# An attention and MLP kernel: casts moved from ScalarE to GpSimd, attention tiles issued in pairs ahead of the MLP, and the last output tile in two banks

## The chip, the cores and the metric

The kernel runs on one core of a Trainium2 chip. The metric is the device time of one execution in microseconds. In the text PE is TensorE (PEld its weight loads), DVE is VectorE, ACT is ScalarE, POOL is GpSimd, SP is SyncE, whose queue issues most DMAs. "fp32r" is the reduced float32 type in which TensorE multiplies faster than in plain float32. L595 means line 595 of the kernel.

## The reference

Sliding-window attention with sink keys, followed by a two-layer MLP, everything in float32 from the outside:

```python
# q, k, v: (4, 8, 768, 64); n_sink = 4, window = 128
scores = q @ k.T / 8
keep = (key < n_sink) | ((0 <= row - key) & (row - key < window))
a = softmax(where(keep, scores, -1e9))
x = (a @ v), heads side by side           # (3072, 512)
h = x @ w_in                              # w_in (512, 2048), given as float64
out = maximum(0.01 * h, h) @ w_out        # w_out (2048, 512), given as float64
```

## The kernel before

**Tiling.** The 3072 tokens are cut into eight units `u` of 384 tokens (half a sequence, T = 3 tiles of 128 rows). A unit is attended in four pairs of heads, then goes through the MLP in 16 chunks `fc` of 128 hidden columns. Precision is kept by splitting: a float32 operand becomes a high part (a cast to fp32r) and a low part (the difference), and a product is three fp32r matmuls: high x high, high x low, low x high. So every weight tile has `hi` and `lo` (L180, L181), every attention output `xh` and `xl` (`emit_x`, L548), every hidden chunk `gh` and `gl` (L604, L605).

**Weights.** They come as float64 and are decoded by three integer instructions on DVE (L172, L174, L176), then cast (ACT) and subtracted (POOL). `load_weights` brings them one tile at a time, alternately of `w_in` and `w_out`.

**Attention of the first two units** (`early_stream`, plain float32 matmuls). A tile is `(u, pair, j)`. Its `score` step is two matmuls (one for each head) into two PSUM banks (`pair_banks`), on DVE the mask, scale and row minimum in one instruction for each head (L303), on ACT the exponential (L305); for `u = 1` also the normalisation on ACT (L484). The probabilities stand in a buffer `pe` of which there are three (`PKB`). Its `turn` step transposes the probabilities on PE into a bank (`tail_pair`, L354, L355), which ACT copies out as `pt` (L357, L360). When the three tiles of a pair have been turned, `gather` (`sinks`) transposes the sink columns, which POOL copied aside (L358), and `value` (`values_pair`) multiplies with V. For `u = 0` the sums are applied after that: POOL spreads them (`rs`, L398), PE transposes them (L431), ACT copies them (L432), DVE multiplies (`xf`, L434), and `emit_x` makes `xh` on ACT (L551) and `xl` on DVE (L552).

**Order.** PE's order is the order in which the program is written; the other engines' instructions are ordered by a planner that simulates the kernel, within the limits of data and buffers. The attention is a generator that yields after every step. The first `early_steps + LEAD0` = 39 steps run ahead of the MLP (`phase[0]` is 0); score tiles then alternate between the bank pairs (s, o0) and (o1, o2), and transposes between banks h and t. Later steps are dealt out between the MLP's steps, at a rate worked out from the step counts. A `turn` follows its `score` by `SAHEAD` = 2 tiles; between the two stand the value group that is pending. Ahead of the MLP stand so 17 scores, 14 turns and the four value groups of unit 0, and four weight tiles are loaded there.

**MLP.** A chunk is 12 matmuls of 384 columns into one bank (L595), then `g` on ACT and DVE (L602, L603), `gh` on ACT, `gl` on POOL for unit 0 and on DVE for the others, and, one chunk later, for each of the three token tiles three matmuls of 512 columns that accumulate into the tile's bank o0, o1 or o2 (L619). After the last chunk the banks are copied out by DVE and stored. For the very last tile the last chunk's three matmuls are made in two halves of 256 columns in the same bank, one half copied by ACT and stored from ACT's queue, the other by DVE and stored from SP's.

Of the kernel before, what the change touches and what calls it, by code (L numbers as in the profile page):

```python
# [9 lines left out]
F32 = mybir.dt.float32  # L10
# [10 lines left out]
P = 128  # L21
# [6 lines left out]
T = 3  # L28
# [13 lines left out]
DEEP = 9.0e8  # L42
SO = 3
LEAD = 12
LEAD0 = 7
SAHEAD = 2
NACT = 4
LAG = 2
# [70 lines left out]
def fast_path(ctx, tc, cpool, qp, qk, vu, vs, w_in, w_out, out, ident, wz, lims, negm, wmin, wmax):  # L119
# [43 lines left out]
    def load_weights():  # L163
        fc, nm = len(wts) // 2, "io"[len(wts) % 2]
        raw = wpool.tile([P, 512, 2], I32, tag=f"w{nm}{fc}", name=f"w{nm}raw{fc}")
        dma = fetch(raw, nm, fc)
        pace(dma, decoded[-DEPTH] if len(decoded) >= DEPTH else anchors[-min(PRED, len(anchors))])
        top, low = raw[:, :, 1], raw[:, :, 0]
        word = ps_t.tile([P, 512], I32, tag="d", name=f"d{nm}{fc}")
        w = iopool.tile([P, 512], F32, tag="io", name=f"w{nm}f{fc}")  # L170
        with tc.issue_after(anchor[0].ins):
            nc.vector.tensor_scalar(out=word, in0=top, scalar1=3, scalar2=0x3FFFFFFF,  # L172
                                    op0=ALU.logical_shift_left, op1=ALU.bitwise_and)
        nc.vector.scalar_tensor_tensor(out=word, in0=top, scalar=-0x40000000, in1=word,  # L174
                                       op0=ALU.bitwise_and, op1=ALU.bitwise_or)
        decoded.append(nc.vector.scalar_tensor_tensor(out=w.bitcast(I32), in0=low, scalar=29, in1=word,  # L176
                                                      op0=ALU.logical_shift_right, op1=ALU.bitwise_or))
        both = wpool.tile([P, 2, 512], F32R, tag=f"w{nm}{fc}", name=f"w{nm}{fc}")
        hi, lo = both[:, 0, :], both[:, 1, :]
        nc.scalar.copy(out=hi, in_=w)  # L180
        nc.gpsimd.tensor_tensor(out=lo, in0=w, in1=hi.bitcast(F32), op=ALU.subtract)  # L181
        wts[nm, fc] = (hi, lo)

# [280 lines left out]
    def early_stream(pend):  # L464
# [2 lines left out]

        def score(u, pair, j):
            if j == 0:
                live[u, pair] = st = dict(raw=raws.pop((u, pair)), v=vraws.pop((u, pair)))  # L470
                load_next(u, pair)
                st["sk"] = apool.tile([P, T, 2, NSK], F32, tag="sk", name=f"sk{u}_{pair}")
                st["sm"] = apool.tile([P, 2, T], F32, tag="sm", name=f"sm{u}_{pair}", bufs=4)
                st["pt"] = apool.tile([P, 2, 2 * TU], F32, tag="pt", name=f"pt{u}_{pair}")
            st = live[u, pair]
            st["w", j] = w = apool.tile([P, 2, W3], F32, tag="pk", name=f"pe{u}_{pair}_{j}", bufs=PKB)
            softmax_pair(u, pair, j, scores_pair(u, pair, j, st["raw"]), w, st["sm"])
            sm = st["sm"][:, :, j] if u else st["sm"]
            if u or j == T - 1:
                nc.vector.tensor_scalar(out=sm, in0=sm, scalar1=1e-9, scalar2=None, op0=ALU.add)  # L480
                nc.vector.reciprocal(out=sm, in_=sm)
            if u:
                for x in range(2):
                    nc.scalar.mul(w[:, x, :], w[:, x, :], st["sm"][:, x, j:j + 1])  # L484
# [6 lines left out]
            live[u, pair]["st"] = sinks(u, pair, live[u, pair]["sk"], live[u, pair])  # L491

        def value(u, pair):
            values_pair(u, pair, live.pop((u, pair)))
            n = u * NPAIR + pair + 2
            if n < EARLY * NPAIR:
                load_values(*divmod(n, NPAIR))

        for k, tile_ in enumerate(tiles):
            score(*tile_)  # L500
            yield
            while pend:
                pend.pop(0)[1]()
                yield
            if k >= SAHEAD:
                u, pair, j = tiles[k - SAHEAD]
                turn(u, pair, j)
                yield
                if j == T - 1:
                    gather(u, pair)  # L510
                    yield
                    pend.append((1, lambda u=u, pair=pair: value(u, pair)))
        for u, pair, j in tiles[len(tiles) - SAHEAD:]:
            pend.append((0, lambda u=u, pair=pair, j=j: turn(u, pair, j)))
        pend.append((0, lambda: gather(u, pair)))
# [32 lines left out]
    def emit_x(u, pair, x):  # L548
        xh = xpool.tile([P, TU], F32R, tag=f"xh{pair}", name=f"xh{u}_{pair}")
        xl = xpool.tile([P, TU], F32R, tag=f"xl{pair}", name=f"xl{u}_{pair}")  # L550
        nc.scalar.copy(out=xh, in_=x)  # L551
        (nc.gpsimd if EARLY <= u < XLP else nc.vector).tensor_tensor(out=xl, in0=x, in1=xh.bitcast(F32), op=ALU.subtract)  # L552
        xs[u].append((xh, xl))

# [23 lines left out]
    def mlp_stream():  # L578
        po = {}
        prev = None  # L580
        for step in range(NU * NFC + 1):
            u, fc = divmod(step, NFC)
            cur = None
            if u < NU:
# [17 lines left out]
                nc.scalar.mul(g, ph[:, 0:TU], 0.01)  # L602
                anchor[0] = nc.vector.tensor_tensor(out=g, in0=ph[:, 0:TU], in1=g, op=ALU.max)  # L603
                nc.scalar.copy(out=gh, in_=g)  # L604
                (nc.gpsimd if u == 0 else nc.vector).tensor_tensor(out=gl, in0=g, in1=gh.bitcast(F32), op=ALU.subtract)  # L605
                cur = (u, fc, gh, gl)
                yield
            if prev is not None:
                v, f, gh, gl = prev
                if f == 0:  # L610
                    po = [ps_o.tile([P, 512], F32, tag=f"o{t}", name=f"o{v}_{t}") for t in range(T)]
                wh, wl = wts["o", f]
                for t in range(T):
                    tsl = slice(t * P, (t + 1) * P)
                    halves = 2 if (v, f, t) == (NU - 1, NFC - 1, T - 1) else 1
                    for x in range(halves):
                        cs = slice(x * 512 // halves, (x + 1) * 512 // halves)
                        for c, (gg, w) in enumerate(((gh, wh), (gh, wl), (gl, wh))):
                            nc.tensor.matmul(po[t][:, cs], lhsT=gg[:, tsl], rhs=w[:, cs], start=f == 0 and c == 0,  # L619
                                             stop=f == NFC - 1 and c == 2 and x == halves - 1)  # L620
                    if f == NFC - 1:
                        last = v == NU - 1 and t == T - 1
                        r0 = (v * T + t) * P
                        if last:
                            obs = [apool.tile([P, 256], F32, tag="stg", name=f"ob{v}_{t}_{x}") for x in range(2)]
                            nc.scalar.copy(out=obs[0], in_=po[t][:, 0:256])
                            nc.scalar.dma_start(out=out[r0:r0 + P, 0:256], in_=obs[0])
                            nc.vector.tensor_copy(out=obs[1], in_=po[t][:, 256:])
                            nc.sync.dma_start(out=out[r0:r0 + P, 256:], in_=obs[1])
                        else:  # L630
                            ob = iopool.tile([P, 512], F32, tag="io", name=f"ob{v}_{t}")
                            nc.vector.tensor_copy(out=ob, in_=po[t])
                            nc.sync.dma_start(out=out[r0:r0 + P, :], in_=ob)
                    yield
            prev = cur
            if u == NU - 1 and fc == NFC // 2:
# [236 lines left out]
```

## Time and profile before

| | us |
|---|---|
| median of 3 runs | 704.83 (704.82 to 705.29) |
| the profiled execution's own time | 704.37 |
| its span, first to last instruction | 702.6 |
| PE busy | 688.7 (98%) |
| DVE busy | 532.1 (76%) |
| ACT busy | 424.2 (60%) |
| POOL busy | 395.1 (56%) |
| mean granted TensorE clock | 0.998 |

A row of the timeline has its start and its length in us, the engine, the line, the operation, output and inputs, and in brackets how long the engine was idle ahead of it and what ended that. A row of the groups has busy time in us and mean nanoseconds of one instruction. A row of the waits has the total in us, how often, and the longest. Numbers behind "xcount" of a merged row span several instructions, so such a row's length is that of all of them.

### The profile page before, as it was taken

To read this page: it belongs to the slowest core of one execution; us is meant where nothing else is said; L and a number is where in the kernel's file an instruction comes from. 1 tells how busy PE (TensorE), PEld (TensorE's weight loads), DVE (VectorE), ACT (ScalarE), POOL (GpSimd) and SP (SyncE) were. 2 spreads that over 40 slices of the span, in tenths; PEclk is the share of its full clock that TensorE was granted. 3 is DMA by queue.
4 is the path that set the end of the run, shared out by engine and by line. 5 is a ranking of instruction groups with operands and counts; after the bars stand their busy time and mean duration, and the time that the engine had idled before them with its cause. 6 is when DMAs were issued, how large, how long until landed. Compare 5 with 4: busy or idle time off the path is not lost.

```text
span 702.6 us, 12490 instructions
## 1 busy us (share of the span) xinstructions
PE 688.7 (98%) x3872; PEld 601.1 (86%) x3872; DVE 532.1 (76%) x1726; ACT 424.2 (60%) x1182; POOL 395.1 (56%) x532
## 2 busy tenths in 40 slices
PE   8999999999999999999999999999999999999995
PEld 5567788898998899999998889998999999988894
DVE  6999898566678888888888898888888877642322
ACT  6987666566666666567566676666566665522221
POOL 3357678454576877576676977667667564400000
PEclk9999999999999999999999999999999999999999
DMA  6865672212215423343333433323332310000001
GB/s 222 285 200 187 210 236 80 91 39 66 73 50 177 139 81 115 91 147 118 121 110 118 150 99 99 120 101 120 125 104 74 117 54 16 2 30 16 1 0 50
DMA packets 42604, 74.33 MB, mean 106 GB/s; under 512 B 3489, under 2 KB 26273, under 8 KB 42529
## 3 DMA queue, kind: packets, MB, share of 16 engines
q1 hardware_dynamic: 42384, 73.31, 32.1%
q8 instruction: 33, 0.54, 0.3%
q14 instruction: 43, 0.34, 0.1%
q10 hardware_dynamic: 144, 0.13, 0.1%
HBM read 67.14 MB, written 6.29 MB: 105 GB/s over the span
## 4 chain that ended last, share of the span: by engine, by line
PE 88%; DVE 3%; ACT 3%; DMA 2%; POOL 1%; issue 1%; SPq 0%; ACTq 0%; DVEq 0%; POOLq 0%
PE h L595 36%; PE o L619 36%; PE v L452 5%; PE s L291 4%; PE t L365 2%; PE v L419 1%; ACT pe L305 1%; PE s L283 1%; DMA vsraw<-in_vs 1%; DMA qkraw<-in_qk 1%; DMA ciraw<-in_w_in 1%; DVE pe L303 1%; PE t L386 0%; PE t L446 0%; DMA lim_raw<-in_lims 0%
## 5 line engine op out<-in xcount | busy, mean ns | idle before, releaser
L595 PE MATMUL h<-xh,wi 128*128 128x384 f32 x1024 | 311.3, 353 | 1.0 <-ACT pt L357 0.5
L619 PE MATMUL o<-wo,gh 128*128 128x512 f32 (+1 forms) x770 | 247.4, 402 | 0.2 <-ACT gh L604 0.2
L595 PEld LDWEIGHTS h<-xh,wi 128*128 128x128 f32 x1024 | 190.0, 188 | 17.5 <-issue 3.3
L595 PE MATMUL h<-xl,wi 128*128 128x384 f32 x512 | 172.9, 338 | 0.3 <-DVE xl L552 0.3
L335 POOL TENSOR_SCALAR_AFFINE_SELECT pt<-stg 128x256 fp32r<-128x256 f32 x240 | 104.4, 459 | 93.5 <-DVE stg L373 71.5
L619 PE MATMUL o<-wo,gl 128*128 128x512 f32 x385 | 152.1, 395 | 0.4 <-POOL gl L605 0.4
L619 PEld LDWEIGHTS o<-wo,gh 128*128 128x128 f32 x770 | 132.6, 189 | 18.6 <-issue 1.3
L603 DVE TENSOR_TENSOR g<-h,g 128x384 f32<-128x384 f32 x128 | 71.1, 555 | 63.4 <-ACT g L602 62.2
L602 ACT ACTIVATE g<-h 128x384 f32<-128x384 f32 x128 | 62.2, 486 | 68.3 <-PE h L595 67.3
L595 PEld LDWEIGHTS h<-xl,wi 128*128 128x128 f32 x512 | 96.9, 189 | 3.6 <-DVE xl L552 0.6
L619 PEld LDWEIGHTS o<-wo,gl 128*128 128x128 f32 x385 | 72.3, 188 | 18.6 <-POOL gl L605 1.1
L604 ACT CAST gh<-g 128x384 fp32r<-128x384 f32 x128 | 65.4, 511 | 32.1 <-DVE g L603 29.4
L605 DVE TENSOR_TENSOR gl<-g,gh 128x384 fp32r<-128x384 f32 x112 | 74.7, 667 | 11.2 <-ACT gh L604 9.5
L320 ACT ACTIVATE pk<-pk,negm 128x128 f32<-128x128 f32 (+1 forms) x144 | 58.2, 404 | 38.0 <-DVE negm L317 37.4
L242 POOL TENSOR_TENSOR qksp<-qkraw,qksp 64x392 fp32r<-64x392 f32 (+1 forms) x48 | 59.4, 1238 | 25.4 <-ACT qksp L241 18.6
L372 ACT CAST stg<-t 128x128 fp32r<-128x128 f32 x120 | 30.9, 258 | 50.1 <-PE t L365 38.7
L291 PEld LDWEIGHTS s<-qksp 128*128 128x128 f32 x288 | 53.2, 188 | 7.7 <-issue 1.1
L291 PE MATMUL s<-qksp 128*128 128x260 f32 (+1 forms) x288 | 56.4, 277 | 0.8 <-DVE negm L317 0.8
L244 POOL TENSOR_TENSOR qksp<-qkraw,qksp 128x384 fp32r<-128x384 f32 x48 | 51.7, 1078 | 3.8
L326 DVE TENSOR_SCALAR pk<-pk,sm 128x132 f32<-128x132 f32 (+1 forms) x120 | 47.6, 396 | 2.1
L452 PEld LDWEIGHTS v<-pt,vsp 128*128 128x128 f32 x336 | 45.0, 189 | 2.6 <-DVE xf L458 0.2
L309 DVE COPY_PREDICATED s<-tri,s 128x128 f32<-128x128 int8 x120 | 34.7, 289 | 16.0 <-PE s L291 14.7
(139 smaller groups left out, 1069.2 us busy)
## 6 DMA issues: line engine op xcount, KB each, us to landing
qkraw<-in_qk SPq DMA_DIRECT2D x24, 454.0 KB, 3.3
qkraw<-in_qk SPq DMA_DIRECT2D x24, 388.0 KB, 3.7
wiraw<-in_w_in SPq DMA_DIRECT2D x16, 512.0 KB, 4.0
woraw<-in_w_out SPq DMA_DIRECT2D x16, 512.0 KB, 3.5
ciraw<-in_w_in SPq DMA_DIRECT2D x16, 512.0 KB, 3.5
coraw<-in_w_out SPq DMA_DIRECT2D x16, 512.0 KB, 3.4
out<-ob SPq DMA_DIRECT2D x23, 256.0 KB, 2.0
vraw<-in_vu SPq DMA_DIRECT2D x14, 256.0 KB, 2.6
```

The source lines that it names most:

```text
L242: nc.gpsimd.tensor_tensor(out=sp[D:P, TU:TU + n], in0=raw[D:P, TU:TU + n], in1=sp[D:P, TU:TU + n].bitcast(F32), op=ALU.subtract)
L244: nc.gpsimd.tensor_tensor(out=sp[:, TU + n:2 * TU + n], in0=raw[:, 0:TU], in1=sp[:, 0:TU].bitcast(F32), op=ALU.subtract)
L291: nc.tensor.matmul(ps[:, 0:kn], lhsT=sp[:, off + j * P:off + (j + 1) * P], rhs=sp[:, TU + k0:TU + k0 + kn], start=c == 0, stop=c == len(pa ...
L320: nc.scalar.activation(out=w, in_=w, func=AF.Exp, scale=-1.0, bias=neg, accum_out=sm)
L335: nc.gpsimd.affine_select(out=out, in_=src, pattern=([[0, x]] if x > 1 else []) + [[sign, P]], base=-1 if prev else 0, channel_multiplier= ...
L452: nc.tensor.matmul(out[:, o:o + m], lhsT=l, rhs=r, start=c == 0, stop=c == len(mms) - 1, skip_group_check=True)
L595: nc.tensor.matmul(ph[:, 0:TU], lhsT=w[:, cs], rhs=x, start=cc == 0 and c == 0, stop=cc == NCC - 1 and c == 2)
L602: nc.scalar.mul(g, ph[:, 0:TU], 0.01)
L603: anchor[0] = nc.vector.tensor_tensor(out=g, in0=ph[:, 0:TU], in1=g, op=ALU.max)
L604: nc.scalar.copy(out=gh, in_=g)
L605: (nc.gpsimd if u == 0 else nc.vector).tensor_tensor(out=gl, in0=g, in1=gh.bitcast(F32), op=ALU.subtract)
L619: nc.tensor.matmul(po[t][:, cs], lhsT=gg[:, tsl], rhs=w[:, cs], start=f == 0 and c == 0, stop=f == NFC - 1 and c == 2 and x == halves - 1)
```

## The change

- `LEAD0` goes from 7 to 6, so 38 steps run ahead of the MLP.
- Ahead of the MLP the cast `hi` of a weight tile is made by POOL instead of ACT.
- For unit 0 `xh` of the first three pairs is made by POOL instead of ACT; the fourth stays on ACT.
- `early_stream` issues, ahead of the MLP, the scores of two tiles one after the other (four banks), then the turns of the two tiles that are due, each followed by its gather and by what is pending. In the MLP it goes tile by tile as before. The V tiles are taken from the table when they are used, no longer with the first score of the pair.
- `gl` of unit 0 is made by POOL only from the third chunk on, by DVE for the first two.
- The last output tile of the last unit accumulates in two banks of 256 columns each (o2 and s) through all 16 chunks. ACT copies the one, DVE the other.

```diff
-LEAD0 = 7
+LEAD0 = 6
...
-        nc.scalar.copy(out=hi, in_=w)
+        if phase[0]:
+            nc.scalar.copy(out=hi, in_=w)
+        else:
+            nc.gpsimd.tensor_copy(out=hi, in_=w)
...
-                live[u, pair] = st = dict(raw=raws.pop((u, pair)), v=vraws.pop((u, pair)))
+                live[u, pair] = st = dict(raw=raws.pop((u, pair)))
...
         def value(u, pair):
+            live[u, pair]["v"] = vraws.pop((u, pair))
...
-        for k, tile_ in enumerate(tiles):
-            score(*tile_)
+        def after(n):
             yield
             while pend:
                 pend.pop(0)[1]()
                 yield
-            if k >= SAHEAD:
-                u, pair, j = tiles[k - SAHEAD]
+            for u, pair, j in n:
                 turn(u, pair, j)
                 yield
+                while pend:
+                    pend.pop(0)[1]()
+                    yield
                 if j == T - 1:
                     gather(u, pair)
                     yield
                     pend.append((1, lambda u=u, pair=pair: value(u, pair)))
+
+        k = 0
+        while k < len(tiles):
+            n = 1 if phase[0] or k % 2 else 2
+            score(*tiles[k])
+            if n > 1:
+                yield
+                score(*tiles[k + 1])
+            yield from after(tiles[max(k - SAHEAD, 0):max(k - SAHEAD + n, 0)])
+            k += n
...
-        nc.scalar.copy(out=xh, in_=x)
+        if u == 0 and pair < NPAIR - 1:
+            nc.gpsimd.tensor_copy(out=xh, in_=x)
+        else:
+            nc.scalar.copy(out=xh, in_=x)
...
-                (nc.gpsimd if u == 0 else nc.vector).tensor_tensor(out=gl, ...)
+                (nc.gpsimd if u == 0 and fc > 1 else nc.vector).tensor_tensor(out=gl, ...)
...
+                    if v == NU - 1:
+                        po[-1] = [(pool.tile([P, 256], F32, tag=tag, name=f"o{v}_{tag}"), slice(x * 256, (x + 1) * 256))
+                                  for x, (pool, tag) in enumerate(((ps_o, "o2"), (ps_s, "s")))]
...
-                    halves = 2 if (v, f, t) == (NU - 1, NFC - 1, T - 1) else 1
+                    for x, (acc, cs) in enumerate(po[t]):
                         for c, (gg, w) in enumerate(((gh, wh), (gh, wl), (gl, wh))):
-                            nc.tensor.matmul(po[t][:, cs], ..., start=f == 0 and c == 0,
-                                             stop=f == NFC - 1 and c == 2 and x == halves - 1)
+                            nc.tensor.matmul(acc, ..., start=f == 0 and c == 0,
+                                             stop=f == NFC - 1 and c == 2)
```

More of the change, by code (lines that the diff above doesn't have):

```diff
@@ L604, in mlp_stream @@
                 nc.scalar.copy(out=gh, in_=g)
-                (nc.gpsimd if u == 0 else nc.vector).tensor_tensor(out=gl, in0=g, in1=gh.bitcast(F32), op=ALU.subtract)
+                (nc.gpsimd if u == 0 and fc > 1 else nc.vector).tensor_tensor(out=gl, in0=g, in1=gh.bitcast(F32), op=ALU.subtract)
                 cur = (u, fc, gh, gl)
@@ L610, in mlp_stream @@
                 if f == 0:
-                    po = [ps_o.tile([P, 512], F32, tag=f"o{t}", name=f"o{v}_{t}") for t in range(T)]
+                    po = [[(ps_o.tile([P, 512], F32, tag=f"o{t}", name=f"o{v}_{t}"), slice(0, 512))] for t in range(T)]
+                    if v == NU - 1:
+                        po[-1] = [(pool.tile([P, 256], F32, tag=tag, name=f"o{v}_{tag}"), slice(x * 256, (x + 1) * 256))
+                                  for x, (pool, tag) in enumerate(((ps_o, "o2"), (ps_s, "s")))]
                 wh, wl = wts["o", f]
@@ L614, in mlp_stream @@
                     tsl = slice(t * P, (t + 1) * P)
-                    halves = 2 if (v, f, t) == (NU - 1, NFC - 1, T - 1) else 1
-                    for x in range(halves):
-                        cs = slice(x * 512 // halves, (x + 1) * 512 // halves)
+                    r0 = (v * T + t) * P
+                    for x, (acc, cs) in enumerate(po[t]):
                         for c, (gg, w) in enumerate(((gh, wh), (gh, wl), (gl, wh))):
-                            nc.tensor.matmul(po[t][:, cs], lhsT=gg[:, tsl], rhs=w[:, cs], start=f == 0 and c == 0,
-                                             stop=f == NFC - 1 and c == 2 and x == halves - 1)
@@ L621, in mlp_stream @@
[L621 to L633, printed above, removed]
+                            nc.tensor.matmul(acc, lhsT=gg[:, tsl], rhs=w[:, cs], start=f == 0 and c == 0,
+                                             stop=f == NFC - 1 and c == 2)
@@ new lines, in mlp_stream @@
+                        if f == NFC - 1:
+                            if len(po[t]) > 1:
+                                ob = apool.tile([P, 256], F32, tag="stg", name=f"ob{v}_{t}_{x}")
+                            else:
+                                ob = iopool.tile([P, 512], F32, tag="io", name=f"ob{v}_{t}")
+                            if len(po[t]) > 1 and x == 0:
+                                nc.scalar.copy(out=ob, in_=acc)
+                                nc.scalar.dma_start(out=out[r0:r0 + P, cs], in_=ob)
+                            else:
+                                nc.vector.tensor_copy(out=ob, in_=acc)
+                                nc.sync.dma_start(out=out[r0:r0 + P, cs], in_=ob)
```

## The prediction

> **What bounds the kernel now.** I read the page's head first, then busy times by stretch, then the waits of the first 45 us, then the timeline where a wait ended late, and last the tail.
>
> ```profile
> PE 688.7 (98%) x3872; PEld 601.1 (86%) x3872; DVE 532.1 (76%) x1726; ACT 424.2 (60%) x1182; POOL 395.1 (56%) x532
> 16.00:34.00 18.00, 16.56 (x123) 9.16 (x122) 17.65 (x65) 17.07 (x56) 6.33 (x11) 1.00 0.85 274
> 34.00:38.80 4.80, 3.98 (x23) 2.67 (x22) 3.81 (x13) 4.80 (x15) 1.59 (x3) 1.00 0.49 160
> 46.00:116.00 70.00, 69.84 (x405) 55.74 (x404) 65.05 (x151) 49.67 (x120) 50.33 (x52) 1.00 0.62 204
> 116.00:600.00 484.00, 482.87 (x2732) 435.48 (x2732) 392.11 (x1347) 310.12 (x890) 321.05 (x431) 1.00 0.31 99
> DVE pe L303 <- PE s L283: 2.9, 5, 0.9
> PEld s L283 <- DMA woraw<-in_w_out: 0.2, 1, 0.2
> ```
>
> The columns of a stretch are its length, then PE, PEld, DVE, ACT and POOL busy, granted clock, DMA share, GB/s. Two regimes stand there. From 46 us on PE is busy 69.84 of 70 and 482.87 of 484 us: there the time is the sum of the matmuls, and only a stall of PE or another matmul counts. Ahead of 38.8 us it isn't: PE's modelled busy time is full of latency, while DVE does 17.65 and ACT 17.07 of the 18 us from 16 to 34. So this kernel has a head set by DVE and ACT together, then a body that is PE alone. Whatever ends the head earlier moves the body forward unchanged, as long as the body doesn't stall. DMA isn't a limit in the head: the one wait laid on a transfer of weights is 0.2 us.
>
> The head ends at the first matmul that uses the last attention pair's `xl`. Followed back:
>
> ```profile
> 32.52 0.55 PE L431 MATMUL t<-ident,rs 128*128 128x128 f32 x3
> 34.24 0.47 ACT L432 COPY rs<-t 128x384 f32<-128x384 f32 x1
> 35.17 0.55 DVE L434 TENSOR_TENSOR xf<-v,rs 128x384 f32<-128x384 f32 x1
> 35.94 0.58 ACT L357 COPY pt<-t 128x512 f32<-128x512 f32 x1
> 36.20 0.43 DVE L303 CUSTOM_DVE_ANT_0 pe<-s,wide 128x260 f32<-128x260 f32 x1
> 36.55 0.42 DVE L303 CUSTOM_DVE_ANT_0 pe<-s,wide 128x260 f32<-128x260 f32 x1
> 36.57 0.44 PE L595 MATMUL h<-xh,wi 128*128 128x384 f32 x1 [0.51 <-ACT pt L357]
> 36.90 0.69 DVE L172 TENSOR_SCALAR di<-wiraw 128x512 int32<-128x512 int32 x1
> 37.37 0.53 ACT L551 CAST xh<-xf 128x384 fp32r<-128x384 f32 x1
> 37.62 0.69 DVE L174 SCALAR_TENSOR_TENSOR di<-wiraw,di 128x512 int32<-128x512 int32 x1
> 38.23 0.55 DVE L552 TENSOR_TENSOR xl<-xf,xh 128x384 fp32r<-128x384 f32 x1
> 38.84 0.44 PE L595 MATMUL h<-xl,wi 128*128 128x384 f32 x1 [0.26 <-DVE xl L552]
> ```
>
> The five links (rs, xf, xh, xl and the transposes) take 0.55 + 0.47 + 0.55 + 0.53 + 0.55 = 2.65 us by themselves; from 32.52 to 38.78 they took 6.26. The other 3.6 us are queues: `rs` waited 1.2 us on ACT, `xh` 1.65 us after `xf` ended at 35.72 on ACT. This is where work taken from ACT is worth something.
>
> **The change part by part.**
>
> *Casts to GpSimd.* Ahead of the MLP the cast `hi` of four weight tiles and `xh` of three pairs leave ACT for POOL.
>
> ```profile
> L180 ACT CAST wi<-wif 128x512 fp32r<-128x512 f32 x3 | 1.8, 616 | 0.3 <-DVE wif L176 0.3
> L180 ACT CAST wo<-wof 128x512 fp32r<-128x512 f32 x2 | 1.2, 625 | 0.0
> L551 ACT CAST xh<-xf 128x384 fp32r<-128x384 f32 x4 | 2.1, 517 | 0.0
> L112 POOL COPY m<-m 128x128 f32<-128x128 f32 x1 | 0.3, 289 | 0.0
> L398 POOL COPY rs<-sm 128x384 f32<-128x384 f32 x4 | 2.0, 504 | 5.3 <-DVE xf L434 3.0 <-DVE sm L481 2.3
> L194 POOL TENSOR_SCALAR zeroo<-mago 128x512 f32<-128x512 f32 x16 | 28.4, 1776 | 1.7 <-ACT mago L192 1.7
> ```
>
> ACT is relieved of 4 x 0.62 + 3 x 0.517 = 4.0 us (the fifth row-180 cast belongs to the MLP and stays). No such cast on POOL is in the trace. The nearest rows are its plain copies, 289 ns at 128 and 504 at 384 columns, a line that gives 0.61 us at 512; the far end is a one-input TENSOR_SCALAR at 1.78. I take the copies: POOL gets 4 x 0.61 + 3 x 0.50 = 3.9 us more, on top of 7.9 us in the 22.8 us from 16 to 38.8. At the far end (4 x 1.78 + 3 x 1.34 = 11.1 us) it would be 19 of 22.8 and still not the longest queue. Queued behind a cast on POOL are the small `sk` and `rs` copies which PE's transposes need; the cover is POOL's idle half, and where that is gone PE pays up to one cast, 0.6 us, a pair.
>
> What does ACT's 4.0 us bring? Not 4.0, since DVE is the other full engine and its work stays. From 16.00 to 38.78 DVE is busy 17.65 + 3.81 = 21.5 us. The shorter lead takes one tile's softmax out of this (36.20 to 36.90, two rows, with reads 0.8 us): 20.7 us, so `xl` can't end ahead of 16.0 + 20.7 = 36.7 while the decode at 36.90 and 37.62 (1.4 us, next weight tile) stands ahead of it, and 35.3 if it comes after. ACT alone would allow 16.0 + (17.07 + 3.9 - 4.0) = 33.0. I take 36.7: either the decode stays, or about as much idle time remains as DVE has there now (0.35 + 0.99 = 1.3 us). That is **-2.1 us**, between 0 (idle time grows) and -3.5.
>
> *Scores of two tiles together.* No instruction is added; PE gets s(k), s(k+1), then the transposes of k-2 and k-1. It goes at the 2.9 us in which DVE waited five times for a score; four of those banks existed before, so the lookahead for DVE isn't longer on average: `pe` has three buffers, hence tile k+1's softmax can only be written once tile k-2's transposes have run, which now stand behind both scores. Up to the value matmuls of the first pair, this order is bounded by ACT's exponentials as before. I put it at 0, between -1.5 (half of the 2.9 us) and the price in the third rival. `vraws.pop` at value time costs nothing: the same DMAs are issued by the same calls. On SP's queue the load of a next pair is issued up to one score earlier, with the transfer of the pair's buffer as before.
>
> *LEAD0 7 to 6.* With the new order 38 steps hold 16 scores, 14 turns and four value groups; the 39 before hold 17, 14 and four. The seventeenth score moves to between the ninth and tenth matmul of the MLP.
>
> ```profile
> 44.54 0.64 PE s L283 x4
> 42.28 1.01 POOL L605 TENSOR_TENSOR gl<-g,gh 128x384 fp32r<-128x384 f32 x1 [0.23 <-ACT gh L604]
> 43.34 0.50 PE L619 MATMUL o<-wo,gl 128*128 128x512 f32 x1 [0.37 <-POOL gl L605]
> L605 DVE TENSOR_TENSOR gl<-g,gh 128x384 fp32r<-128x384 f32 x1 | 0.6, 558 | 0.6 <-ACT gh L604 0.6
> ```
>
> It is 0.64 us of PE, hidden if PE gets there before `xl` (nine matmuls begun at 36.57 were waiting for a bank that ACT's copy at 35.94 freed, itself late in ACT's queue). I charge half: **+0.3** (0 to 0.64).
>
> *`gl` of the first two chunks on DVE.* 0.56 us in place of POOL's 1.01, and PE stood at 43.34 for exactly this: **-0.4** (-0.45 to +0.7, a decode instruction queued ahead on DVE). But DVE then carries 2 x 0.56 and the seventeenth softmax, 0.8 + 0.3, in a stage where it is busy 65.05 of 70. The slack of 5 us hides it on the whole; short waits of PE for `g` I put at **+0.3** (0 to 1).
>
> *The last output tile in two banks.*
>
> ```profile
> 693.28 0.63 PE L619 MATMUL o<-wo,gh 128*128 128x512 f32 x2
> 693.98 0.40 PE L619 MATMUL o<-wo,gh 128*128 128x256 f32 x2
> 694.58 0.28 PE L619 MATMUL o<-wo,gl 128*128 128x256 f32 x1
> 694.95 0.37 ACT L626 COPY ob<-o 128x256 f32<-128x256 f32 x1 [2.65 <-PE o L619]
> 695.42 0.43 DVE L628 COPY ob<-o 128x256 f32<-128x256 f32 x1 [0.55 <-ACT ob L626]
> 696.01 0.39 SPq L629 DMA_DIRECT2D out<-ob  x1
> ```
>
> Today ACT waits for the last matmul of both halves and DVE for ACT. With a bank each, DVE starts at 694.95: -0.47 us. The price: three 512-column matmuls take 693.98 - 693.28 = 0.70 us, six halves 0.72 (0.12 between starts, 694.58 + 0.12 the end), so 15 chunks x 0.02 = +0.3 us. Together **-0.2** (-0.5 to +0.3).
>
> Sum: -2.1 + 0.3 - 0.4 + 0.3 - 0.2 = **-2.1 us**. The profiled execution took 704.37 us (span 702.6 and 1.8 around it), which becomes 702.3; the median of the runs, 704.83, lies 0.46 above it and becomes **702.7 us**.
>
> **The rivals.**
>
> *Head without idle (700.6 us).* The planner of the other engines moves the decode behind `xl` and ACT's free time keeps DVE fed: `xl` ends at 35.3, -3.5, the score is hidden, the rest -0.7. For it: ACT was 100% busy from 34 to 38.8. Against: DVE was idle 0.35 us in all from 16 to 34, so little can be squeezed.
>
> *The shared path of DVE and POOL (704.8 us).* [...]
>
> ```profile
> 28.79 1.28 POOL L181 TENSOR_TENSOR wi<-wif,wi 128x512 fp32r<-128x512 f32 x1
> 29.57 0.91 DVE L552 TENSOR_TENSOR xl<-xf,xh 128x384 fp32r<-128x384 f32 x1
> ```
>
> The same instruction took 0.55 us at 38.23, when POOL stood still: 0.36 more. With POOL half again as busy, four `xl` and two `gl` each pay 0.36: +2.1 us on the engine that bounds the head and the gain is gone. [...] Against this rival: three of four `xl` met nothing, and a pair's `xl` follows its own cast.
>
> *DVE blocked by its own buffers (709 us).* If DVE's queue has softmax k+1 ahead of other work, DVE stands until the exponential (and scaling) of tile k-2 and its transposes are through, with decodes, `xf` and `xl` queued behind. Price: the longest such wait, 0.9 us, in each of seven pairs = 6.3 us, less 2.1: 709.0. It makes the kernel slower by over 0.2% once a pair costs over (2.1 + 1.4) / 7 = 0.5 us. For it: three buffers for four tiles in flight. Against: the decodes are other work that can be put in between.
>
> **How the numbers follow.** 0.2% is 1.4 us, about what a measurement here tells from no change. Likeliest sum 0.48 (701.5 to 703.3 by itself), head without idle 0.15, shared path 0.23, blocked DVE 0.14. Faster is 0.48 + 0.15 = 0.63, within 0.2% 0.23, slower 0.14. From 700.6 to 705.9 leaves out most of the last case and the lower edge of the second, under 2 in 10.
>
> **What would show it.** Row 180 and 551 casts on POOL near 0.61 and 0.50 us; `rs` within 0.3 us of its transposes; the first `h<-xl` that waited at 38.84 near 36.7; no wait of a second over 42 to 44 us; ACT and DVE copies at the end starting less than 0.4 us apart. It is wrong if DVE's idle time ahead of 36 us grows past 1.3 us, if POOL's casts take 1.5 us or more and PE's transposes wait for POOL, or if PE after 46 us shows new gaps over 1 us in sum.

## The result, and the profile after

| | before | after |
|---|---|---|
| median of 6 runs each, same chip | 704.91 us (703.01 to 705.42) | 709.12 us (708.11 to 711.09) |
| the profiled execution's own time | 704.37 us | 709.17 us |
| its span | 702.6 us | 707.5 us |

The ratio is 1.0059, with a 95% interval of 1.0047 to 1.0071: the change costs 4.2 us. The prediction was 702.7 us with 700.6 to 705.9 as its range, so it has the wrong sign and the time lies outside.

The head of the page of the changed kernel, then the stretches of time that the prediction read, for the changed kernel (length, then busy us of PE, PEld, DVE, ACT and POOL, granted clock, DMA share, GB/s):

```profile
PE 687.1 (97%) x3917; PEld 604.9 (85%) x3917; DVE 536.1 (76%) x1728; ACT 421.1 (60%) x1175; POOL 398.1 (56%) x537
...
16.00:34.00 18.00, 14.17 (x111) 9.15 (x109) 17.19 (x58) 13.14 (x45) 9.86 (x16) 1.00 0.74 244
34.00:38.80 4.80, 2.98 (x28) 1.91 (x24) 4.80 (x17) 4.15 (x13) 1.48 (x5) 0.99 0.78 202
38.80:46.00 7.20, 7.14 (x32) 6.01 (x32) 5.40 (x17) 5.82 (x17) 3.04 (x4) 0.77 0.41 130
46.00:116.00 70.00, 67.87 (x382) 53.72 (x383) 66.32 (x151) 49.09 (x118) 47.63 (x49) 1.00 0.64 204
```

ACT was relieved as planned: 13.14 us busy from 16 to 34 us, where it was 17.07. Nothing came of it: PE is busy 14.17 us there instead of 16.56, and the clock, 1.00 everywhere in the rows of before, is 0.77 from 38.8 to 46 us. From 46 to 116 us PE now lacks 2.13 us, where it lacked 0.16: new gaps of over 1 us there were one of the signs by which the prediction said it would be wrong.

The waits of PE up to 36 us, of the changed kernel (total us, how often, longest):

```profile
PE t L358 <- ACT pt L360: 3.0, 2, 1.5
PE t L389 <- ACT pt L360: 2.0, 2, 1.5
```

PE waits 5.0 us for ACT's copies `pt`, although ACT has less to do. The timeline of the changed kernel shows why, and how the head ends:

```profile
27.29 1.27 POOL L184 TENSOR_TENSOR wo<-wof,wo 128x512 fp32r<-128x512 f32 x1
27.43 1.15 DVE L483 TENSOR_SCALAR sm<-sm 128x6 f32<-128x6 f32 x1
...
30.79 0.51 POOL L567 CAST xh<-xf 128x384 fp32r<-128x384 f32 x1 [0.20 <-DVE xf L437]
31.71 1.27 POOL L184 TENSOR_TENSOR wi<-wif,wi 128x512 fp32r<-128x512 f32 x1
31.74 1.26 DVE L483 TENSOR_SCALAR sm<-sm 128x2 f32<-128x2 f32 x1
...
36.73 0.61 POOL L183 CAST wo<-wof 128x512 fp32r<-128x512 f32 x1 [2.01 <-DVE wof L176]
36.92 0.46 ACT L435 COPY rs<-t 128x384 f32<-128x384 f32 x1
37.44 0.33 PE L357 MATMUL t<-ident,pe 128*128 128x128 f32 x1 [1.19 <-ACT rs L435]
38.72 0.69 PE L613 MATMUL h<-xh,wi 128*128 128x384 f32 x1 [0.63 <-ACT pt L360]
39.20 0.52 PE L613 MATMUL h<-xl,wi 128*128 128x384 f32 x1
41.10 0.55 DVE L570 TENSOR_TENSOR xl<-xf,xh 128x384 fp32r<-128x384 f32 x1
41.90 0.80 PE L286 MATMUL s<-qkp 64*128 64x260 f32 x4
42.84 0.43 DVE L306 CUSTOM_DVE_ANT_0 pe<-s,wide 128x260 f32<-128x260 f32 x1 [1.19 <-POOL wi L184]
42.90 0.34 PE L613 MATMUL h<-xl,wi 128*128 128x384 f32 x1
```

POOL's casts cost what was expected (0.51 and 0.61 us). But the small addition to the sums (L483, 0.14 to 0.17 us at its seven other places up to 46 us) starts just behind a POOL subtraction and ends with it, twice: 1.15 and 1.26 us. `xl` of the last pair ends at 41.65 us, where it was 38.78 and 36.7 was forecast. A matmul of 384 columns takes 0.52 us up to 42 us and 0.34 after it: PE runs at half clock there (0.50 granted from 38.7 to 42.1 us). And the seventeenth score, moved into the first chunk, stands at 41.90.

The body is no longer free of stalls. Two places of the timeline of the changed kernel, at 85 and at 398 us:

```profile
82.79 1.31 POOL L184 TENSOR_TENSOR wo<-wof,wo 128x512 fp32r<-128x512 f32 x1
83.12 0.99 DVE L483 TENSOR_SCALAR sm<-sm 128x2 f32<-128x2 f32 x1 [0.92 <-ACT pe L308]
86.08 0.47 ACT L620 ACTIVATE g<-h 128x384 f32<-128x384 f32 x1
87.97 0.45 PE L613 MATMUL h<-xh,wi 128*128 128x384 f32 x1 [1.55 <-DVE g L621]
...
397.35 1.28 POOL L259 TENSOR_TENSOR vsp<-vraw,vsp 128x512 fp32r<-128x512 f32 x1
397.40 1.64 DVE L623 TENSOR_TENSOR gl<-g,gh 128x384 fp32r<-128x384 f32 x1
399.87 0.48 PE L294 MATMUL s<-qksp 128*128 128x260 f32 x2 [1.54 <-DVE negm L320]
```

In both a DVE instruction is stretched beside a POOL subtraction (0.99 us against 0.14 to 0.17, 1.64 against 0.56), and PE later stands about 1.5 us for DVE. At 398 us that is the row minimum, one instruction behind; at 88 us it is `g`, up to which DVE has worked without a pause since the addition, so the link there is read from the order and not tested by itself.

Where PE stood in the profiled executions (us at which these matmuls start; the numbers in brackets count the first layer's matmuls):

| kernel | first (1) | third chunk (25) | (769) | (961) | last of the second layer |
|---|---|---|---|---|---|
| before | 36.57 | 45.92 | 375.60 | 460.02 | 694.58 |
| after | 38.72 | 49.19 | 380.06 | 466.50 | 700.70 |
| shorter lead alone (i1) | 36.53 | 49.95 | 379.43 | 464.16 | 697.98 |
| paired order, old lead (i2) | 38.57 | 47.75 | 376.23 | 460.91 | 695.06 |
| casts alone (e2) | 38.60 | 49.00 | 378.22 | 464.60 | 698.60 |
| casts, no addition (f2) | 36.32 | 46.58 | 376.41 | 462.85 | 696.52 |
| after with the old lead (j1) | 40.26 | 49.38 | 379.13 | 465.57 | 699.41 |

From the last of these matmuls to the end of the span, 6.5 to 8.2 us passed in the kernels tried (both the shortest and the longest in a kernel with the two-bank end), so differences below 1 us are read from the medians and not from one span.

### The profile page after: what moved, and what is told of

Its sections match the earlier page's. It is cut to its first block, busy times and chain, and to the rows that moved or that the text cites. A ratio compares the mean times of both kernels' runs of the same rounds, so it can differ in the third digit from the quotient of the medians.

```text
span 707.5 us, 12580 instructions
## 1 busy us (share of the span) xinstructions
PE 687.1 (97%) x3917; PEld 604.9 (85%) x3917; DVE 536.1 (76%) x1728; ACT 421.1 (60%) x1175; POOL 398.1 (56%) x537
## 4 chain that ended last, share of the span: by engine, by line
PE 86%; DVE 7%; ACT 2%; DMA 2%; issue 1%; POOL 1%; SPq 0%; DVEq 0%; POOLq 0%; ACTq 0%
PE h L613 35%; PE o L639 34%; PE v L455 5%; PE s L294 4%; PE t L368 2%; PE v L422 1%; ACT pe L308 1%; DVE pe L306 1%; PE o_s L639 1%; PE o_o L639 1%; DMA vsraw<-in_vs 1%; PE s L286 1%; DVE gl L623 1%; DMA ciraw<-in_w_in 1%; PE t L449 0%
## 5 line engine op out<-in xcount | busy, mean ns | idle before, releaser
L639 PE MATMUL o<-wo,gh 128*128 128x512 f32 x736 | 237.3, 403 | 0.5 <-ACT gh L622 0.5
L639 PE MATMUL o<-wo,gl 128*128 128x512 f32 x368 | 145.5, 395 | 0.2 <-DVE gl L623 0.2
L639 PEld LDWEIGHTS o<-wo,gh 128*128 128x128 f32 x736 | 126.1, 189 | 18.5 <-issue 2.5
L623 DVE TENSOR_TENSOR gl<-g,gh 128x384 fp32r<-128x384 f32 x114 | 77.5, 680 | 11.2 <-ACT gh L622 9.5
L639 PEld LDWEIGHTS o<-wo,gl 128*128 128x128 f32 x368 | 69.1, 188 | 17.5 <-DVE gl L623 0.8
```

The source lines that it names most:

```text
L623: (nc.gpsimd if u == 0 and fc > 1 else nc.vector).tensor_tensor(out=gl, in0=g, in1=gh.bitcast(F32), op=ALU.subtract)
L639: nc.tensor.matmul(acc, lhsT=gg[:, tsl], rhs=w[:, cs], start=f == 0 and c == 0, stop=f == NFC - 1 and c == 2)
```

## The experiments

Every kernel is compared with the kernel before on the same chip; on the chips used that took 705.0 to 705.5 us. Numbers in brackets behind a ratio are its 95% interval; a cost in us is the ratio less one, times 705.

**The parts alone.** Each is the kernel before with one part of the diff above.

```diff
e1_order:  LEAD0 = 6, early_stream in pairs, vraws.pop in value()
e2_casts:  hi on nc.gpsimd ahead of the MLP, xh of three pairs of unit 0 on nc.gpsimd
e3_tail:   last tile accumulated in two banks
e5_gl:     gl of the first two chunks on nc.vector
e4_no_order: the changed kernel with LEAD0 = 7 and the old early_stream
```

> The kernel before with the paired order alone (scores of two tiles together, V taken at use, 38 steps ahead of the MLP); casts, gl and the last tile as before. Theory 'order': the pair order alone lengthens the head, since softmax k+1 waits for the transposes of tile k-2 and the value group stands behind two turns; the time is 3 to 5 us over the kernel before, and the first matmul that waits for xl stands 3 us or more later than 38.84. [...]

> The kernel before with the casts of the head moved to POOL and nothing else. Theory 'casts': 3 to 5 us slower than before, with DVE's small sm instructions ahead of 36 us at over 1 us where POOL's subtraction runs beside them. Theory 'order': within 1 us of before or up to 2 us faster, since ACT is relieved of 4.0 us while the order of PE stays.

> The kernel before with the last output tile in two banks and nothing else. All theories: faster by 0.7 to 1.1 us; the end comes about 1.2 us sooner after the last matmul (the profile of the changed kernel has 6.8 us there, the one before 8.0), and the 45 more matmuls cost 0.2 to 0.3 us.

> The changed kernel with the old order (tile by tile, 39 steps); casts on POOL, gl and last tile as changed. Theory 'order': all of the loss goes, 702.5 to 704. Theory 'casts': still 707 to 709.

> The kernel before with gl of the first two chunks on DVE and nothing else. If the sums of the earlier runs hold (casts +1.9, last tile -1.7, both with gl +1.5), gl on DVE costs 1 to 1.5 us; by the prediction's term it gains 0.4 and costs 0.3, no change within 0.7 us. The wait for gl at 43.34 should go in both cases.

| | median, us (runs) | ratio to before |
|---|---|---|
| e1_order | 707.50 (12) | 1.0026 [1.0013, 1.0040] |
| e2_casts | 707.25 (12) | 1.0028 [1.0015, 1.0042] |
| e3_tail | 703.68 (12) | 0.9975 [0.9963, 0.9987] |
| e4_no_order | 706.87 (12) | 1.0022 [1.0009, 1.0035] |
| e5_gl | 705.22 (12) | 1.0002 [0.9992, 1.0012] |

So two parts are slower by about 2 us each, the casts and what e1 changes. The two banks bring 1.8 us, and `gl` on DVE nothing. That nothing isn't the absence of an effect. In e5's trace PE waits longer for the first `gl` than in the kernel before, 0.70 us against 0.37, since a decode stands ahead of it on DVE:

```profile
43.59 0.51 PE L619 MATMUL o<-wo,gl 128*128 128x512 f32 x1 [0.70 <-DVE gl L605]
```

Its matmul (961) starts at 461.91, 1.89 us later than before, its last one at 695.86, 1.28 us later, and the end follows 6.94 us after that, where it was 7.99.

In the casts' timeline the mechanism of the head stands without the new order (e2_casts):

```profile
34.02 0.87 POOL L183 CAST wo<-wof 128x512 fp32r<-128x512 f32 x1 [0.43 <-DVE wof L176]
34.35 0.58 DVE L483 TENSOR_SCALAR sm<-sm 128x2 f32<-128x2 f32 x1
35.22 0.91 ACT L487 ACTIVATE pe<-pe,sm 128x260 f32<-128x260 f32 x2 [0.58 <-DVE sm L484]
36.55 0.33 PE L357 MATMUL t<-ident,pe 128*128 128x128 f32 x1 [2.08 <-ACT rs L435]
...
395.48 1.28 POOL L259 TENSOR_TENSOR vsp<-vraw,vsp 128x512 fp32r<-128x512 f32 x1
395.54 1.64 DVE L611 TENSOR_TENSOR gl<-g,gh 128x384 fp32r<-128x384 f32 x1
```

DVE's addition is stretched beside POOL's cast, ACT's scaling (L487) stands 0.58 us for the sums, ACT's copy `rs` stands behind the scaling in ACT's queue (the transposes that it copies end at 33.37, it starts at 36.04), and PE waits 2.08 us for `rs`. ACT's freed time has become idle time of a queue that keeps its order: from 6.8 us to the end of the last `xl` it is idle 5.6 us here, 2.2 in the kernel before. Most of the difference is the exponential's wait for DVE's row minimum (first row e2_casts, second the kernel before; the longest, 5.1 us in both, is the first one and lies mostly ahead of 6.8 us):

```profile
ACT pe L308 <- DVE negm L306: 8.4, 9, 5.1
ACT pe L305 <- DVE negm L303: 6.1, 5, 5.1
```

The seven additions up to the last `xl` take 2.91 us against 1.15. And `xl` isn't what PE stands for here: it ends at 38.25, 0.5 us sooner than before, but PE comes to the MLP 2.0 us later and uses it first at 41.16, without a wait.

**Three tries on PE's waits in the paired order.** They took the 5 us for `pt` at face value: if the order is slow because PE waits there, taking away what it waits for should help.

```diff
f1_order_buf4:    e1_order + a fourth buffer for probabilities ahead of the MLP
f5_order_gatherv: e1_order + the gather's transposes into bank v in place of h or t
g1_order_vlate:   e1_order - "while pend: pend.pop(0)[1](); yield" behind each turn
```

> The paired order alone, with a fourth buffer for the probabilities ahead of the MLP (every fourth tile takes the place of a weight tile that is loaded late). Theory 'three buffers' (softmax k+1 waits for the turn of k-2): the loss of the order goes, within 0.7 us of before. Theory 'two transpose banks' (two turns, a gather and the sums' transposes in a row wait for ACT's copies out of banks h and t): no change against the order alone, 1.5 to 2.5 us over before, with the waits of PE for the pt copies (1.6 us at 26.2) still there.

> The paired order alone, with the sink columns' transpose ahead of the MLP in the values' bank v instead of h or t, so that a bank is needed from h and t only four times a pair. Theory 'two transpose banks': PE's waits for the pt copies shrink from 3.1 us to under 1.5 and the time comes 1 us or more nearer to before. Theory 'three buffers': no change against the order alone.

> The paired order alone, with the value group put behind the next two scores instead of between the turns and those scores. Theory 'value ahead of the scores' (DVE and ACT starve while PE runs the value matmuls, as at 26.2 to 30.3 where DVE waited 1.9 us for a score): the loss of the order falls by 1.5 us or more, to within 0.7 us of before. Theory 'two turns in a row wait for ACT's copies': the loss stays at 1.5 to 2.5 us, with PE's waits for pt as with the order alone.

They took 709.84 us (8 runs, 1.0071 [1.0048, 1.0095]), 707.94 (6, 1.0037 [1.0024, 1.0049]) and 707.52 (7, 1.0047 [1.0028, 1.0066]). None gives the time back; the waits only change their names. PE's waits in f5_order_gatherv:

```profile
PE v L419 <- DVE ste L393: 2.6, 2, 2.1
PE h L607 <- DVE xl L564: 1.8, 1, 1.8
PE t L354 <- ACT rs L432: 1.3, 2, 0.9
```

With f1 the prediction's third rival falls too, though its 709 us came closest to the measured time: a fourth buffer doesn't help, and in the changed kernel DVE waits only 0.4 us in all, from 6.8 to 42 us, for a turn's transposes, where the rival had 6.3. That its number came out is luck. (f1 is itself slower than e1 by 3.2 us; no run shows why.)

**The lead apart from the pairs.** e1 had changed two things at once, and the constant had not been tried by itself.

```diff
i1_lead6:       before,        -LEAD0 = 7  +LEAD0 = 6   (nothing else)
i2_order_lead7: e1_order,      -LEAD0 = 6  +LEAD0 = 7
j1_after_lead7: after,         -LEAD0 = 6  +LEAD0 = 7
```

> The kernel before with LEAD0 = 6 alone, so that 38 steps in the old order run ahead of the MLP. If the shorter lead is what the paired order pays for: 706.5 to 707.5 us. If the pairing is: within 0.5 us of the kernel before, since one step (a score's two matmuls, 0.64 us of PE) only moves behind the start of the MLP.

> The paired order and the later use of the V tiles with LEAD0 left at 7, so that 39 steps run ahead. If the pairing is what costs: 707 us or more, as with 38 steps (707.5). If the shorter lead is: near the kernel before, 705.3.

> The changed kernel with LEAD0 = 7 in place of 6 and nothing else. If the shorter lead makes the change slow, because the seventeenth tile's softmax, exponential and scaling then stand ahead of the first chunk's g and gh: 2.4 us off the changed kernel as in the paired order alone, 706.7 us, or down to 705.5. If the casts' own cost (2.0 us) and the order's waits make it slow whatever the lead is: 708.5 us or more.

| | median, us (runs) | ratio to before |
|---|---|---|
| i1_lead6 | 709.10 (6) | 1.0047 [1.0033, 1.0060] |
| i2_order_lead7 | 705.07 (12) | 0.9995 [0.9987, 1.0004] |
| j1_after_lead7 | 706.78 (12) | 1.0024 [1.0013, 1.0035] |

The constant alone costs 3.3 us (2.3 to 4.2), the paired order with the old constant nothing that can be told, and in the changed kernel the constant is worth 2.5 us of the 4.2 (1.0059 against 1.0024). PE's waits up to 46 us in i2_order_lead7 are the very ones that e1 has (3.1, 1.7 and 1.2 us in both):

```profile
PE t L355 <- ACT pt L357: 3.1, 2, 1.6
PE t L354 <- ACT rs L432: 1.7, 2, 1.3
PE t L386 <- POOL rs L398: 1.2, 1, 1.2
```

They make the MLP start 2.0 us later (first column of the table above), but at the last matmul only 0.5 us is left. The longest waits of a trace are not what the change costs.

What one score behind the ninth matmul does is in the timeline of i1_lead6 (the row at the end is the kernel before, for the matmul of 44.77):

```profile
38.29 0.71 PE L283 MATMUL s<-qkp 64*128 64x260 f32 x4
38.97 1.44 POOL L181 TENSOR_TENSOR wi<-wif,wi 128x512 fp32r<-128x512 f32 x1 [2.29 <-ACT wi L180]
39.19 1.25 DVE L480 TENSOR_SCALAR sm<-sm 128x2 f32<-128x2 f32 x1
40.95 0.42 DVE L303 CUSTOM_DVE_ANT_0 pe<-s,wide 128x260 f32<-128x260 f32 x1
41.41 0.51 ACT L305 ACTIVATE pe<-pe,negm 128x260 f32<-128x260 f32 x1 [0.94 <-DVE negm L303]
42.30 0.55 DVE L603 TENSOR_TENSOR g<-h,g 128x384 f32<-128x384 f32 x1
42.41 0.90 ACT L484 ACTIVATE pe<-pe,sm 128x260 f32<-128x260 f32 x2
43.22 0.56 ACT L357 COPY pt<-t 128x512 f32<-128x512 f32 x1
44.20 0.51 ACT L604 CAST gh<-g 128x384 fp32r<-128x384 f32 x1
44.77 0.72 PE L619 MATMUL o<-wo,gh 128*128 128x512 f32 x2 [2.30 <-ACT gh L604]
46.68 0.69 PE L619 MATMUL o<-wo,gl 128*128 128x512 f32 x1 [1.19 <-POOL gl L605]
...
42.25 0.72 PE L619 MATMUL o<-wo,gh 128*128 128x512 f32 x2 [0.16 <-ACT gh L604]
```

The score itself is 0.64 us of PE and hidden, as charged. What isn't hidden is its train: the softmax on DVE stands at 40.95 us in place of 36.20, ahead of `g`; its exponential, the scaling and `pt` stand on ACT ahead of the first chunk's `gh`. `gh` starts at 44.20, and PE, which began the MLP at the same moment as before (36.53 against 36.57), waits 2.30 us for it, then 1.19 for `gl`; in the kernel before the two waits were 0.16 and 0.37. The third chunk starts 4.03 us late, with the clock at half from 46.8 to 50.2 us.

Two more things are in that trace. DVE's addition at 39.19 takes 1.25 us beside the subtraction of 38.97, where the next one (43.36) takes 0.15, so about 1.1 us of the train's delay is this stretch again. And of the 4.06 us that the way from the first matmul to the third chunk is longer, 2.70 are waits of PE and 1.37 are longer busy time, which is the half clock. All six executions of i1 have a mean granted clock of 0.992 to 0.995; 126 executions of the kernel before on the chips of these experiments have 0.996 to 0.999. The traces without a half-clock stretch ahead of the end have 0.996 to 0.999, those with one 0.994 to 0.996, those with two 0.991 and 0.992. By these traces, then, each execution of i1 has at least one, and a part of the 3.3 us is the clock's; how much of the median, no run separates. In the paired order the lead costs at like clocks too: the executions with 0.996 or more mean 706.5 us in e1 (6) and 704.8 in i2 (7).

In the changed kernel the same constant is paid elsewhere. The first of the rows below is the stretch from 46 to 116 us of j1_after_lead7, the second its one wait of PE there:

```profile
46.00:116.00 70.00, 69.83 (x402) 56.09 (x402) 65.38 (x155) 49.45 (x121) 49.23 (x51) 1.00 0.69 213
...
PE h L613 <- DVE g L621: 0.2, 1, 0.2
```

Against the changed kernel's 67.87 us PE is busy 1.96 us more; the stall at 87.97 us, 1.55 us, is gone.

**The small addition.** If its stretch beside POOL is what the casts cost, leaving it out should pay. These kernels leave out the addition of 1e-9 to the softmax sums of the first two units.

```diff
f2_casts_noadd (e2_casts), i3_after_noadd (after), j2_after_lead7_noadd (j1):
-                nc.vector.tensor_scalar(out=sm, in0=sm, scalar1=1e-9, ..., op0=ALU.add)
g2_casts_noadd_skact: f2 +
-            nc.vector.tensor_copy(out=sk[:, 0:nj, h % 2], ...)   # late units
+            nc.scalar.copy(out=sk[:, 0:nj, h % 2], ...)
```

> The casts on POOL alone, without the instruction on DVE that adds 1e-9 to the softmax sums of the first two units (the sum is at least 1, so float32 does not see it). With the casts on POOL seven of these took 2.9 us in place of 1.15, at most 1.2 us each. Theory 'DVE shut out by POOL': xl of the fourth pair ends 1.5 us or more sooner than 38.25, and the time falls by 1 us or more against the casts alone, to 706 or less. Theory 'ACT's order' (the copy of the spread sums stands in ACT's queue behind scalings that wait for DVE): under 0.7 us, since the queue's order stays.

> The casts on POOL, without the 1e-9, and with the late units' copy of the sink columns (12 columns, on DVE) made by ACT. In all kernels with the casts on POOL, and in no other, PE stood 1.9 us near 395 us behind a gl of 1.64 us; ahead of it this copy took 1.29 us beside a subtraction of POOL, where it takes 0.17 alone. Theory 'who starts first': without this copy on DVE the stand at 395 goes and the time falls by 1.5 us or more against the same kernel with the copy on DVE (706.2), to below before. If the stand stays, the copy wasn't its origin.

> The changed kernel without the addition of 1e-9 to the sums (DVE) for the first two units. If that addition, shut out by POOL's subtractions, delays ACT's queue here as with the casts alone: 1.0 us or more off the changed kernel, 708 us or less. If the paired order's own waits for banks cover it: no change, 709 us.

> The changed kernel with LEAD0 = 7 and without the addition of 1e-9 to the sums for the first two units. If lead and addition add up: below 704 us, as the rest of the change (two banks at the end, 1.7 us) would then be what is left. If both act through the same delay of the first gh: as with either of them alone, 705.5 to 706.5 us.

| | median, us (runs) | ratio to before |
|---|---|---|
| f2_casts_noadd | 706.21 (12) | 1.0011 [1.0002, 1.0021] |
| g2_casts_noadd_skact | 704.90 (12) | 0.9998 [0.9984, 1.0012] |
| i3_after_noadd | 705.70 (12) | 0.9999 [0.9988, 1.0011] |
| j2_after_lead7_noadd | 707.89 (8) | 1.0036 [1.0022, 1.0051] |

Without it the casts cost 1.2 us less (the two intervals still touch) and the changed kernel 4.2 us less, which is all that the change had cost. But with the old lead its removal makes the kernel 0.8 us slower, within the intervals, and brings nothing, so it doesn't add up, and neither of j2's two expectations held. Part of the answer is the clock. j2's executions fall in two groups: three with a mean granted clock of 0.998 or 0.999 took 706.1 to 706.4 us, five with 0.995 or 0.996 took 707.8 to 708.5. In e2_casts those with 0.997 or more mean 706.2 us (5) and the others 707.9 (7); f2_casts_noadd, with eleven of twelve in the upper group, means 706.1 there. So about half of e2's loss of 2 us goes with a half-clock stretch that falls in some executions and not in others, and in f2 it hardly ever does. In the kernel before, whose mean clock stays between 0.996 and 0.999, the 45 executions at 0.996 mean 705.5 us and the 81 above 705.2, so within that band the mean says little by itself. Why j2 falls into the stretch more often than j1 is open.

Beside it stands the stall near 395 us: from matmul 769 to 961 e2 takes 86.4 us and before 84.4, and f2 takes 86.4 too. g2 was to remove it by moving the copy that stood ahead of `gl`. It took 0.9 us less, within the intervals, yet the stall remained (1.59 us between the starts of two matmuls, from 393.9), so that explanation failed. It stands in all eleven kernels with the casts on POOL or the early `gl` on DVE, also in g1, and in none of the other seven nor in before. From 132 us on the instructions of DVE, ACT and POOL come in the same order in all of these but those with the sink copy on ACT; which of two neighbours on different engines starts first is what differs. What decides that is open, and so is what the stall costs in the end: e5 and g2 have it and take no longer than the kernel before.

**Keeping the clock up.** Four extra matmuls of 384 columns ahead of the second turn of each pair, on zeros, into bank v.

```diff
f4_after_warm: after +
+    if (u, pair, j) == n[-1]: keep_warm(4)   # 4 matmuls into a spare tile of ps_v
```

> The changed kernel with four more matmuls of zeros ahead of the second turn of every pair of tiles in the head, which have no use but to keep PE active. Theory 'clock': the stretch of 3.4 us at half clock (38.7 to 42.1) goes, the mean clock is 0.998 in most runs, and the time falls by 1 to 1.5 us against the changed kernel, to about 707.6. If the clock costs nothing, the time stays or grows by the matmuls' own 0.6 us a pair where PE is on the path.

It took 709.96 us (6 runs, 1.0057 [1.0042, 1.0073]). The half-clock stretch was gone from its trace (mean granted clock 0.997, 0.995 in the changed kernel's), but PE waited 4.1 us for bank v to be free for the extra matmuls, so this prices nothing.

**Towards a better kernel.**

```diff
g4_tail_skact: e3_tail + the copy of the sink columns on ACT (as in g2)
g3_best:       g4 + gl of the first two chunks on DVE, without the addition of 1e-9
```

> A version that might beat both: the kernel before with the last tile in two banks and the late units' copy of the sink columns on ACT. The last tile alone brought 1.7 us; DVE loses 24 copies of 0.17 to 1.3 us in a stage where PE waits little, so 0 to 1 us more: 702.5 to 703.7, against 705.3 before. If ACT's longer queue delays gh or the pt copies, 704 to 705.

> The kernel before with the last tile in two banks, the first two chunks' gl on DVE, no addition of 1e-9 for the first two units, and the late copy of the sink columns on ACT. If these add up: the two-bank tail with the sink copy on ACT gave 702.1 us, gl nothing, the missing addition at most 0.3 us of DVE ahead of the MLP, so 701.5 to 702.3. If the stall of 1.5 us near 395 us comes with it, as with the other kernels that make gl early on DVE: 703.5.

g4_tail_skact took 702.13 us (9 runs, 0.9958 [0.9945, 0.9971]): faster than both kernels, by 3.0 us against before. The sink copy on ACT was expected to cost 0 to 1 us beside e3_tail and came out 1.2 us to the good, with intervals that touch. g3_best took 703.61 (8 runs, 0.9973 [0.9962, 0.9983]). It has the stall near 393 us (1.60 us between two starts) and g4 hasn't; the medians lie 1.5 us apart, as the expectation had it for that case.

## Why the prediction was wrong

**The shorter lead: the wrong term.** "It is 0.64 us of PE, hidden if PE gets there ... I charge half: +0.3". Measured +3.3 us by itself, 2.5 us in the changed kernel. The step priced what moved on PE and left out what follows from it on DVE and ACT: softmax and sums on DVE, exponentials, scaling and `pt` on ACT stand in their queues ahead of the first chunk's `g` and `gh` (in i1 `g` ends at 42.85 and `gh` starts at 44.20). The first chunk is where PE has no other work to go on with, so their delay is PE's; a half-clock stretch behind it adds a share. The next step, "+0.3 (0 to 1)" for DVE's load, touched it, but counted slack on the whole stretch from 46 us, when the price falls due in one place at 42 to 47 us.

**The head as a sum of DVE's work: the wrong form, and the larger miss.** "`xl` can't end ahead of 36.7 ... I take 36.7": -2.1 us. Measured +2.0 us for the casts, 4.1 us off, with `xl` at 38.25 in e2 and at 41.65 in the changed kernel. The step failed twice. DVE's work was taken at its old lengths, but the additions grew by 1.8 us beside POOL. And the end of `xl` was taken for the end of the head: in e2 `xl` comes 0.5 us sooner and the MLP starts 2.0 us later, since PE stands 2.08 us for `rs`. What ACT was to gain (4.0 us) it did gain, and spent it idle, 7.3 us up to the last `xl` of the changed kernel against 2.2: its queue kept its order (in e2 it stood idle 0.58 us for the sums of a scaling, while `rs`, whose transposes had ended at 33.37, came behind), so the freed time went only to whatever stood at its head, and that was mostly an exponential waiting for DVE's row minimum, a copy `rs` waiting for PE, and now and then a scaling waiting for DVE's sums.

**The shared path: a rival that counted too little.** The second rival let `xl` and `gl` pay beside POOL, 0.36 us each, worked out from the one `xl` of 0.91 us, and nothing else. The runs show the stretch for the small addition as well: 0.14 to 0.17 us elsewhere, 1.15 and 1.26 beside a subtraction. The one that starts at 27.43 ends at 28.58, the subtraction of 27.29 at 28.56. The rival's arithmetic left the additions out. That a shared path is behind it, no run shows.

**Paired scores: 0, right, in part by luck.** 0.9995 with the lead unchanged, though by a way that was not foreseen: 2.0 us late into the MLP, 0.5 at its end.

**`gl` on DVE: -0.4 and +0.3, right in sum by luck.** 1.0002. The gain of 0.4 isn't there: PE's wait for the first `gl` grew by 0.33 us, by the decode that the term's upper end had named, and most of the stall near 395 us that its trace shows was made up for by a shorter end.

**Two banks: the right sign, too small, and mostly not for the reason given.** -0.2 (-0.5 to +0.3) forecast, -1.8 measured (-2.6 to -0.9). The rows of the changed kernel's end:

```profile
700.70 0.28 PE L639 MATMUL o_s<-wo,gl 128*128 128x256 f32 x1
700.71 0.37 ACT L647 COPY ob<-o_o 128x256 f32<-128x256 f32 x1 [2.29 <-PE o_o L639]
701.08 0.42 DVE L650 COPY ob<-o_s 128x256 f32<-128x256 f32 x1
```

DVE's copy starts 0.38 us behind the last matmul's start, 0.84 before: the 0.46 us that was forecast. The other 1.3 us don't lie at the end: e3's last store leaves SP no earlier after the last matmul (1.59 us, 1.44 before), and the span ends 8.21 us after it, 7.99 before. In the profiled executions e3's last matmul starts at 693.18, 1.40 us sooner than before, and all of that has been gained by 486 us, although up to 632.9 us the two kernels have the same instructions in the same order on every engine. So most of this gain isn't the two banks' work; where it comes from is open, and it warns that kernels can differ by over 1 us for no reason that their edit gives.

**The sum.** Casts +2.0, lead +2.5 (in its place), pairs -0.4, `gl` +0.1, two banks -1.8: +2.4 us, against 4.2 (3.3 to 5.0). The missing 1.8 us appear where the parts meet: j1, with all but the lead, is +1.7 us where its parts alone give -0.1. e4, with neither pairs nor lead, has most of it already: +1.6 us, where casts, `gl` and two banks give +0.3. Which of these three meet was not separated; and as each part's interval is 0.6 to 1 us wide to either side, what is missing is hardly clear of the noise.

## What to carry to other kernels

Price a moved step by the whole train behind it, on every engine whose queue keeps its order, as ACT's did here, and at the place where the first consumer has nothing else to do; a constant that moves one tile cost more here than the new order it came with. Time taken off an engine is worth nothing while the head of its queue waits: ACT was relieved of 4.0 us here and stood idle 5.1 us longer. Try every constant of a change by itself before explaining the longest waits of the trace: here these waits stood unchanged in a kernel that lost nothing.

## What was unexpected of the hardware

- A DVE addition over 128x2 numbers takes 0.14 to 0.17 us, and 1.26 beside a POOL subtraction over 128x512 that started 0.03 us earlier; DVE's `gl` takes 1.64 us beside one of 1.28, against 0.56 alone.
- PE's clock fell to half (0.50 granted) for stretches of 3.4 us: 38.7 to 42.1 us in the changed kernel, 46.8 to 50.2 in i1. The longest wait of PE ahead of these two was 1.5 and 2.3 us. The traces of ten kernels have twelve such stretches ahead of the end; the longest gap of PE ahead of any was 2.3 us, and in the 3.4 us ahead of each PE was busy 26 to 53% of the time. The kernel before, e3, e5, g3 and g4 have none, and there PE is busy 74% or more of any 3.4 us from 10 to 60 us. f2, f4, g2, i2 and j2 have none either, though each has 3.4 us with PE busy 46 to 53%. So in these traces a half-idle 3.4 us always stood ahead of a stretch, and didn't always bring one. It comes and goes: up to the MLP PE has the same program in e1 and i2 but for one score, and e1's trace has the stretch at 26.7 us, i2's none. What decides it was not shown.
- Between groups with and without such a stretch lie 1.7 us in e2 and 1.9 in j2, about what half speed over 3.4 us would cost by estimate (3.4 / 2 = 1.7).
